# Token rows of attention sent to DRAM from ScalarE's queue instead of SyncE's

## The chip, the cores and the metric

The kernel runs on one core of a Trainium2 chip. The metric is the device time of one execution in microseconds (us). Engines are named PE (TensorE), DVE (VectorE), ACT (ScalarE), POOL (GpSimd) and SP (SyncE); SP computes nothing here, it issues transfers. A transfer issued from SP goes to one hardware queue (q1 in the profile), one issued from ACT to another (q10), one from POOL to a software queue (q0).

## The reference, cut to what matters

Attention with a sigmoid in place of the softmax, then a mixture of experts with one expert per token, then a dense two-layer block:

```python
scores = q @ k.T / sqrt(64) - log(448)         # batch 4, 12 heads, 448 tokens, head size 64
x = sigmoid(scores) @ v                        # -> 1792 tokens of 768
e = argmax(x @ w_gate); g = max of softmax     # 8 experts
x[token] = g * (relu(x[token] @ w1[e]) @ w2[e])  # 768 -> 1024 -> 768
out = relu(x @ w_in)**2 @ w_out                # 768 -> 2048 -> 768
```

## The kernel before

**Three stages.** Attention runs over 24 units, one for each pair of heads in each batch (`units`, numbered n = 0 to 23). Routing then sorts the tokens by expert. The mixture of experts and the dense block follow, with all their weights streamed from DRAM. Routing needs the router's logits of every token, so nothing of the later stages can begin on PE before the last unit's token rows have been projected.

**One unit.** A unit n issues, in program order: the load of unit n+3 (L133, L134, both on SP); four score groups `score` on PE, each followed by a sigmoid on ACT (L158) that frees one of two PSUM buffers; between them the product with v (`av`, L164 and L167) of unit n-1, in steps c = 0, 1, 3, 2; and between step 3 and step 2 a call of `rows` for unit n-2. After step 2 of unit n-1, DVE copies the result out of PSUM (`fin_av`, L171, tile xT). Units also carry DVE and ACT work that packs the dense weights (L90 to L97), stored from POOL (L98).

**`rows`.** PE transposes the finished 128x448 block of a unit to token rows and multiplies it by the router's weights at once (L177, PSUM tile pt, one buffer). ACT copies the result to SBUF (L179, tile xn, two buffers). A transfer writes the token rows to the DRAM tensor x_d (L180: 448 rows of 512 bytes, 224 KB). DVE adds the logits to lg (L183, L185). Because xn has two buffers, the copy L179 for unit m may begin only when the transfer L180 for unit m-2 has landed.

**Order.** The whole program is under a manual schedule: every engine, and every engine's transfer issues, run in program order. On SP an issue that waits therefore holds all issues behind it. Up to unit 20, the load of unit n+3 waits until unit n-1's v has been read, which is the end of unit n. From unit 20 on there are also two loads of 768 KB of expert weights per unit into the same four buffers:

```python
if n >= len(units) - 4:
    rawb.append(rawp.tile([128, 2 * CH], F32, tag="raw", name=f"raw{n}", bufs=4))
    ...
        nc.sync.dma_start(out=raw[c], in_=wm[0, :, len(raw) + c])   # L241
```

The buffer that `raw{n}` takes is that of unit n's own q, k and v, which are last read by `av` in unit n+1. These two loads stand ahead of the call of `rows` for unit n-2 in SP's order.

After unit 23, `rows` for unit 22, the four steps of `av` for unit 23 and `rows` for unit 23 are run, and then routing begins on DVE with a maximum over lg (L304). Tokens of a slot are gathered from x_d by POOL (L446).

Of the kernel before, what the change touches and what calls it, by code (L numbers as in the profile page):

```python
# [20 lines left out]
B, H, S, D = 4, 12, 448, 64  # L21
# [6 lines left out]
CP = 112  # L28
# [28 lines left out]
def moe_kernel(ctx: ExitStack, tc: tile.TileContext, qk, v, wg, wm, w2, out):  # L57
    nc = tc.nc
# [6 lines left out]
    x_d = dram.tile([NT + 128, DM], F32, name="x_d")  # L65
# [41 lines left out]
    with ExitStack() as actx:  # L107
# [65 lines left out]
        def rows(b, j):  # L173
            pt = ps_e.tile([128, 2, 512], F32, tag="pt", name=f"pt_{b}_{j}")
            xn = sp_.tile([128, NC, IW], F32, tag="xn", name=f"xn_{b}_{j}")
            for c in range(NC):
                nc.tensor.matmul(pt[:CP, c // 2, (c % 2) * IW:(c % 2) * IW + IW], xT[b, j][:, c * CP:(c + 1) * CP], iw[:, j, :],  # L177
                                 start=True, stop=True, skip_group_check=True)
            nc.scalar.activation(xn[:CP].rearrange("p (a c) n -> p a (c n)", a=2), pt[:CP, :, :2 * IW], AF.Copy)  # L179
            nc.sync.dma_start(out=x_d[128 + b * S:128 + (b + 1) * S, j * 128:(j + 1) * 128].rearrange("(c p) d -> p c d", p=CP), in_=xn[:CP, :, :128])  # L180
            l = lg[:, b * NC:(b + 1) * NC, :]
            if j == 0:
                nc.vector.tensor_copy(l, xn[:CP, :, 128:])  # L183
            else:
                nc.vector.tensor_tensor(l, l, xn[:CP, :, 128:], op=ALU.add)  # L185
# [6 lines left out]
        def extras():  # L192
            rows(*done.pop(0))
# [240 lines left out]
    with ExitStack() as mctx:  # L434
# [141 lines left out]
        for step in FIRST.split():  # L576
            c = int(step[1])
# [208 lines left out]
```

## Time and profile before

| | |
|---|---|
| median of 3 runs | 1073.06 us (1071.05 to 1073.38) |
| the profiled execution's own time | 1073.23 us |
| its span in the trace | 1071.6 us |
| mean granted clock of PE | 0.981 of full speed |
| attention, first instruction to last logits | 0 to 197.7 us |

The profile names a group of instructions by line, engine and tiles. The span starts with the first instruction; all times of rows are microseconds from there. "[2.33 <-DMA x_d<-xn]" behind a row says that the engine stood idle for 2.33 us just before, until the named thing released it. Granted clock is the share of its full rate that PE was allowed: 1.00 is 2.4 GHz, 0.50 is 1.2 GHz.

### The profile page before, as it was taken

To read this page: it belongs to the slowest core of one execution; us is meant where nothing else is said; L and a number is where in the kernel's file an instruction comes from. 1 tells how busy PE (TensorE), PEld (TensorE's weight loads), DVE (VectorE), ACT (ScalarE), POOL (GpSimd) and SP (SyncE) were. 2 spreads that over 40 slices of the span, in tenths; PEclk is the share of its full clock that TensorE was granted. 3 is DMA by queue.
4 is the path that set the end of the run, shared out by engine and by line. 5 is a ranking of instruction groups with operands and counts; after the bars stand their busy time and mean duration, and the time that the engine had idled before them with its cause. 6 is when DMAs were issued, how large, how long until landed. Compare 5 with 4: busy or idle time off the path is not lost. (4 is left out here: it accounts for less than half of the span.)

```text
span 1071.6 us, 14446 instructions
## 1 busy us (share of the span) xinstructions
PE 1016.4 (95%) x5502; PEld 858.0 (80%) x5502; DVE 631.8 (59%) x565; ACT 639.0 (60%) x757; POOL 188.8 (18%) x132
## 2 busy tenths in 40 slices
PE   7999998179999999999999999999999999999997
PEld 3555554068888888889888889998889988899997
DVE  3777774597888888888885567432432323313351
ACT  5666664367888888888875575225652256522661
POOL 0000000373425344252421000001000010000100
PEclk9999998689999999999999999999999999999999
DMA  8788988466149164614445456534242342422550
GB/s 277 265 296 287 319 296 281 137 255 253 45 164 366 60 228 142 221 45 152 173 133 204 141 211 229 174 98 138 89 148 89 118 147 89 147 89 89 194 190 30
DMA packets 50104, 187.80 MB, mean 175 GB/s; under 512 B 6576, under 2 KB 17328, under 8 KB 47984
## 3 DMA queue, kind: packets, MB, share of 16 engines
q1 hardware_dynamic: 45008, 161.03, 44.0%
q0 software_dynamic: 4944, 25.56, 6.2%
q8 instruction: 45, 0.74, 0.3%
q10 hardware_dynamic: 80, 0.25, 0.1%
q14 instruction: 27, 0.22, 0.1%
HBM read 230.85 MB, written 31.47 MB: 245 GB/s over the span
## 5 line engine op out<-in xcount | busy, mean ns | idle before, releaser
L358 DVE TENSOR_TENSOR wl<-raw,wh 128x1536 fp32r<-128x1536 f32 x126 | 256.2, 2056 | 51.5 <-ACT wh L357 49.1
L357 ACT ACTIVATE wh<-raw 128x1536 fp32r<-128x1536 f32 x144 | 213.7, 1484 | 2.8 <-ACT wh L357 0.2
L358 DVE TENSOR_TENSOR wrl<-raw,wrh 128x1536 fp32r<-128x1536 f32 x43 | 75.6, 1758 | 133.2 <-ACT wrh L357 133.1
L476 PE MATMUL py<-wh,hl 128*128 128x384 f32 x304 | 104.7, 345 | 6.2 <-DVE hl L504 6.2
L158 ACT ACTIVATE a<-sc,bias_s 128x896 f32<-128x896 f32 x96 | 82.9, 915 | 42.8 <-PE sc L154 42.7
L474 PE MATMUL py<-wh,hh 128*128 128x384 f32 x304 | 106.8, 351 | 0.0
L475 PE MATMUL py<-wl,hh 128*128 128x384 f32 x304 | 103.1, 339 | 0.1
L714 PE MATMUL pq<-wrh,sh 128*128 128x384 f32 x296 | 99.9, 338 | 0.0
L358 POOL TENSOR_TENSOR wl<-raw,wh 128x1536 fp32r<-128x1536 f32 x18 | 64.1, 3561 | 201.7 <-ACT wh L357 201.7
L716 PE MATMUL pq<-wrh,sl 128*128 128x384 f32 x296 | 99.4, 336 | 0.0
L715 PE MATMUL pq<-wrl,sh 128*128 128x384 f32 x296 | 99.3, 336 | 0.0
L676 PE MATMUL pp<-yh,wrh 128*128 128x512 f32 (+1 forms) x264 | 95.8, 363 | 2.7 <-PEq L623 2.7
L678 PE MATMUL pp<-yh,wrl 128*128 128x512 f32 (+1 forms) x264 | 95.9, 363 | 0.0
L677 PE MATMUL pp<-yl,wrh 128*128 128x512 f32 (+1 forms) x264 | 95.7, 363 | 0.0
L357 ACT ACTIVATE wrh<-raw 128x1536 fp32r<-128x1536 f32 x43 | 63.8, 1483 | 50.3 <-PE pq L716 43.2
L474 PE MATMUL ph<-wh,xh 128*128 128x512 f32 x228 | 92.6, 406 | 0.3 <-ACT xh L460 0.3
L476 PE MATMUL ph<-wh,xl 128*128 128x512 f32 x228 | 90.6, 397 | 0.0
L475 PE MATMUL ph<-wl,xh 128*128 128x512 f32 x228 | 90.4, 396 | 0.0
L680 ACT ACTIVATE r<-pp 128x512 f32<-128x512 f32 (+1 forms) x64 | 34.8, 544 | 86.2 <-PE pp L678 86.2
L358 DVE TENSOR_TENSOR rl<-raw,rh 128x1536 fp32r<-128x1536 f32 x21 | 36.9, 1759 | 75.8 <-ACT rh L357 75.8
L476 PEld LDWEIGHTS py<-wh,hl 128*128 128x128 f32 x304 | 57.6, 189 | 11.7 <-DVE hl L504 11.7
L164 PE MATMUL po<-a,qkv 128*64 128x448 f32 x288 | 66.2, 567 | 0.0
(168 smaller groups left out, 2047.7 us busy)
## 6 DMA issues: line engine op xcount, KB each, us to landing
raw<-in_wm SPq DMA_DIRECT2D x160, 768.0 KB
raw<-w_d SPq DMA_DIRECT2D x62, 768.0 KB
cs<-in_w SPq DMA_DIRECT2D x11, 1536.0 KB
qkv<-in_qk SPq DMA_DIRECT2D x23, 480.0 KB
w_d<-cd POOLq DMA_DIRECT2D x11, 768.0 KB, 8.8
raw<-in_w SPq DMA_DIRECT2D x5, 1536.0 KB
y_d<-y SPq DMA_DIRECT2D x19, 384.5 KB
qkv<-in_v SPq DMA_DIRECT2D x24, 256.0 KB
```

The costliest lines, as they stand in the source:

```text
L158: nc.scalar.activation(a[:, :n], ps[:, :n, :S], AF.Sigmoid, bias=bias_s, scale=1.0 / math.sqrt(D))
L357: nc.scalar.activation(h, src, AF.Copy)
L358: (nc.gpsimd if pool else nc.vector).tensor_tensor(l, src, f32(h), op=ALU.subtract)
L474: nc.tensor.matmul(ps, lh, rh, start=first, stop=False)
L475: nc.tensor.matmul(ps, lh, rl, start=False, stop=False)
L476: nc.tensor.matmul(ps, ll, rh, start=False, stop=last)
L676: nc.tensor.matmul(pp[:, :N], lh, rh, start=(k == 0), stop=False)
L677: nc.tensor.matmul(pp[:, :N], lh, rl, start=False, stop=False)
L678: nc.tensor.matmul(pp[:, :N], ll, rh, start=False, stop=(k == KD - 1))
L714: nc.tensor.matmul(po[t][:, :384], lh, wc[:, o:o + 384], start=(g == 0), stop=False)
L715: nc.tensor.matmul(po[t][:, :384], lh, wcl[:, o:o + 384], start=False, stop=False)
L716: nc.tensor.matmul(po[t][:, :384], ll, wc[:, o:o + 384], start=False, stop=(g == KF2 - 1))
```

## The change

The 24 transfers of token rows to x_d (L180) are issued from ACT's queue, directly behind the copy L179 that fills xn, and no longer from SP's. Nothing else is different: same size, same shape, same buffers, same place in the program.

```diff
             nc.scalar.activation(xn[:CP].rearrange("p (a c) n -> p a (c n)", a=2), pt[:CP, :, :2 * IW], AF.Copy)
-            nc.sync.dma_start(out=x_d[128 + b * S:128 + (b + 1) * S, j * 128:(j + 1) * 128].rearrange("(c p) d -> p c d", p=CP), in_=xn[:CP, :, :128])
+            nc.scalar.dma_start(out=x_d[128 + b * S:128 + (b + 1) * S, j * 128:(j + 1) * 128].rearrange("(c p) d -> p c d", p=CP), in_=xn[:CP, :, :128])
```

## Rows read from the trace of the kernel before

**Rows 1.** The page: busy time of each engine.

```profile
PE 1016.4 (95%) x5502; PEld 858.0 (80%) x5502; DVE 631.8 (59%) x565; ACT 639.0 (60%) x757; POOL 188.8 (18%) x132
```

**Rows 2.** Waits up to 230 us: who waited, total us, times, longest.

```profile
ACT xn L179 <- DMA x_d<-xn: 21.7, 4, 10.7
...
DVE qkh L141 <- DMA qkv<-in_qk: 6.8, 1, 6.8
```

**Rows 3.** Timeline of an undisturbed unit: start, duration, engine, line, tiles.

```profile
68.05 0.62 ACT L179 ACTIVATE xn<-pt 112x544 f32<-112x544 f32 x1 [0.75 <-ACT a L158]
...
69.72 1.91 ACT L158 ACTIVATE a<-sc,bias_s 128x896 f32<-128x896 f32 x2 [1.05 <-PE sc L154]
...
71.88 0.19 PEld L154 LDWEIGHTS sc<-qkh 64*128 64x128 f32 x2 [0.70 <-ACT a L158]
...
72.67 0.19 PEld L156 LDWEIGHTS sc<-qkh 128*128 128x128 f32 x1 [0.30 <-issue]
```

**Rows 4.** Timeline of SP's issues at the end of attention.

```profile
171.63 0.65 SPq L180 DMA_DIRECT2D x_d<-xn  x1
...
178.90 0.38 SPq L180 DMA_DIRECT2D x_d<-xn  x1
188.97 0.80 SPq L241 DMA_DIRECT2D raw<-in_wm  x2
189.87 7.90 SPq L180 DMA_DIRECT2D x_d<-xn  x3
```

**Rows 5.** Timeline of ACT at the end of attention.

```profile
171.44 0.63 ACT L179 ACTIVATE xn<-pt 112x544 f32<-112x544 f32 x1 [2.33 <-DMA x_d<-xn]
171.97 1.90 ACT L158 ACTIVATE a<-sc,bias_s 128x896 f32<-128x896 f32 x2
...
179.93 0.62 ACT L179 ACTIVATE xn<-pt 112x544 f32<-112x544 f32 x1 [3.73 <-DMA x_d<-xn]
185.45 0.62 ACT L179 ACTIVATE xn<-pt 112x544 f32<-112x544 f32 x1 [4.90 <-DMA x_d<-xn]
196.82 0.62 ACT L179 ACTIVATE xn<-pt 112x544 f32<-112x544 f32 x1 [10.74 <-DMA x_d<-xn]
```

**Rows 6.** Timeline of PE and DVE at the end of attention.

```profile
172.05 1.72 PE L164 MATMUL po<-a,qkv 128*64 128x448 f32 x8
...
173.70 0.19 PEld L154 LDWEIGHTS sc<-qkh 64*128 64x128 f32 x2 [0.70 <-ACT a L158]
...
175.22 0.91 PE L167 MATMUL po<-a,qkv 128*128 128x448 f32 x2
...
175.97 1.09 PE L177 MATMUL pt<-iw,xT 128*112 128x136 f32 x8
...
176.99 0.97 PE L164 MATMUL po<-a,qkv 128*64 128x448 f32 x4
...
180.69 0.62 DVE L171 COPY xT<-po 128x448 f32<-128x448 f32 x1
...
181.46 2.13 PE L177 MATMUL pt<-iw,xT 128*112 128x136 f32 x8 [3.50 <-DVE xT L171]
...
197.47 0.19 DVE L185 TENSOR_TENSOR lg<-lg,xn 112x32 f32<-112x32 f32 x1 [7.87 <-ACT xn L179]
```

**Rows 7.** Line 180: duration of an issue, ns, shortest/median/longest.

```profile
L180 SPq DMA_DIRECT2D x_d<-xn x24: 305/382/956, 26.6 to 197.5; - x24
```

**Rows 8.** Timeline of the start: ACT's one issue, SP's longest.

```profile
0.94 0.56 ACTq L131 DMA_DIRECT2D qkv<-in_qk  x1
...
7.87 3.52 SPq L220 DMA_DIRECT2D cs<-in_w  x1
```

**Rows 9.** Windows of 2 us: engines' busy time, then PE clock, DMA share, GB/s.

```profile
182.00:184.00 2.00, 2.00 (x9) 1.53 (x10) 0.98 (x1) 0.00 (x0) 0.72 (x2) 0.50 0.94 353
...
216.00:218.00 2.00, 1.81 (x4) 1.45 (x5) 1.83 (x3) 2.00 (x4) 0.00 (x0) 0.50 0.95 348
```

**Rows 10.** Timeline after routing: the first gather of token rows.

```profile
207.20 2.41 POOL L446 DMA_INDIRECT xg<-x_d,idx  x1 [1.39 <-DMA raw<-in_wm]
```

## The prediction

> **What bounds the kernel now.** I read the page first, then the list of waits for the attention stage, then the timelines of SP, ACT and PE around the longest waits, and last the granted clock there. The page [rows 1] shows PE busy for 95% of the span, so only what leaves PE idle, or slows it, can be won back. The list of waits up to 230 us [rows 2] has one entry that concerns the moved transfer: the copy L179 waits four times, 21.7 us in total, for x_d to land. VectorE's wait for a q/k load stands there once only, at the start.
>
> The reader is to see three things in the timelines. First, an undisturbed unit is paced by PE: its rows repeat every 7.27 us (71.88 [rows 3] to 173.70 [rows 6] is 101.82 us, 14 units of 7.27), and between the copy L179, which ends at 68.67, and the next sigmoid at 69.72 ACT stands idle for 1.05 us waiting for PE [rows 3]. Second, the four waits lie in a row at the end of attention, at 171.44, 179.93, 185.45 and 196.82, with 2.33, 3.73, 4.90 and 10.74 us of idle ACT ahead of them [rows 5]. Third, SP's order causes them. The copy for unit 21 ends at 180.55 [rows 5], but its transfer is issued at 189.87, straight behind the weight loads that SP could not issue before 188.97 [rows 4], because their buffer is freed by the last `av`. Those 9.3 us are not transfer time: the data lies ready in SBUF and SP stands at another instruction. From issue to the next copy released by it the transfer then takes 171.63 to 179.93 = 8.3, 178.90 to 185.45 = 6.55, and 189.87 to 196.82 = 6.95 us [rows 4, 5].
>
> The last of these waits is on the path that sets the end: the copy for unit 23 cannot start, the logits are complete only after 197.47 [rows 6], and routing, the gathers and all expert work follow from there.
>
> **The change part by part.** *Removed:* 24 issues on SP, about 0.38 us each [rows 7], 9 us in all. SP is not on the path by its busy time, so this alone is worth nothing; SP's loads may be issued some 0.4 us earlier per unit, and nobody waits for them [rows 2]. Worth nothing too.
>
> *Added:* 24 issues on ACT, each behind the copy that it reads. After 21 of them (units 0 to 20) a sigmoid of the next unit is queued. The trace has no issue of this shape on ACT. From below its cost is zero; the nearest rows are the same transfer on SP, 0.31 to 0.96 us [rows 7], and ACT's one issue, 0.56 us [rows 8]. The idle gap of 1.05 us [rows 3] holds all of these, so I take zero, with that idle time as the cover. If the gap were exceeded, a second cover follows: the first pair of sigmoids runs 69.72 to 71.63, and the fourth score group, which needs the second one's buffer, loads at 72.67 [rows 3], 1.04 us later. That this cover is real is seen at 171.97: these sigmoids start 0.43 us late (69.72 plus 14 units is 171.54), held up by the late copy [rows 5], and the third score group still loads on time at 173.70 [rows 6]. So an issue costs PE nothing up to about 2.1 us.
>
> *Moved:* the transfer is issued as soon as its copy has finished. It passes, on SP's side, the loads of q, k and v, the loads of packed weights and, in the last four units, the expert weights with their long waits. No wait on ACT is new except for its own copy. In the middle of attention this gains nothing, since no copy waits there. At the end I replay the order with the rows' own durations. The last PE step before the disturbance, `av` step 2 in unit 23, ends at 176.99 + 0.97 = 177.96, and the projection for unit 21 at 175.97 + 1.09 = 177.06 [rows 6]. Then:
>
> - copy for unit 21: 0.1 after the projection, 0.62 long: 177.78. The transfer that it needs, that of unit 19, was issued at its own copy, two units (14.5 us) before; the longest delay seen is 8.3 us. No wait.
> - DVE: logits 0.19 [rows 6], then xT for unit 22, 0.62: 178.64; PE follows 0.15 later (180.69 + 0.62 to 181.46 [rows 6]): 178.79.
> - projection for unit 22, 1.02 to the next PE step (175.97 to 176.99): 179.81.
> - `av` of unit 23: steps 0 and 1, 1.65 (172.05 to 173.70); step 3, 0.75 (175.22 to 175.97); step 2, 0.97: 183.18 [rows 6].
> - xT for unit 23, 0.67 with its start: 183.85; projection from 184.00, 1.09: 185.09; copy, 0.72: 185.81; last logits at 185.84.
>
> The copy for unit 22, at about 179.9, needs the transfer of unit 20, issued near 170.6: 9.3 us, more than any delay seen. The copy for unit 23, at 185.2, needs the transfer of unit 21, issued near 177.8. By the delays above that lands between 184.4 and 186.1, so the copy waits for 0 to 0.9 us. I take zero, because the three delays were measured on transfers queued behind 1.5 MB of expert weights issued just ahead, and here the transfer is issued before those of its unit.
>
> The last logits thus move from 197.47 to 185.84: **11.6 us**. Of the four waits nothing comes back later: the transfer of unit 23, issued at 185.8, is down by 194.1 at the longest delay; the first gather, at 207.20 now [rows 10], moves to 195.6. The same reckoning is the cover for routing and the expert stage: all that follows hangs on the logits and moves with them. The time is 1073.23 - 11.6 = 1061.6 us by the profiled execution, which is 0.17 above the median: **1061.5 us**.
>
> *The clock.* PE was granted half its rate (0.50, 1.2 GHz) at 182 to 184 [rows 9], after the idle 3.5 us ahead of 181.46, and the same projection took 2.13 instead of 1.09 us [rows 6]. In the replay that idle time shrinks to 0.8 us (177.96 to 178.79), so I count full rate. If the half rate came all the same, the stretch from that projection to the end of `av` would take what it takes now, 181.46 to 188.97 = 7.5 us [rows 4, 6], instead of 4.4: a loss of 3.1. The first expert matmuls also run at half rate now (216 to 218, [rows 9]); they do so after a pause of the same length, and I take no change. If the rate returned at once some 1 us would be won; if 3 us later, some 1.5 lost.
>
> **The rivals.** *B, part of the gain.* The half rate stays (3.1) and the copy for unit 23 waits (0.9): 1061.5 + 4.0 = 1065.5 us, with the later clock 1067. For it speaks that PE still has pauses; against it that the pause shrinks to a quarter.
>
> *C, nothing happens:* the transfers land as late as before, since it is the engines that are full; 1073.1 us. In the 2 us around 183 their share is 0.94 [rows 9], which speaks for it. Against it: the transfer of unit 21 would have to take 18 us from 177.8 to about 196, while the delays are 6.55 to 8.3 us [rows 4, 5]; and the 9.3 us before its issue are SP's.
> The Trainium skill has a rule of this kind ("DMA: Bandwidth & Descriptors", section "Issuing engines are not separate DMA queues"): transfers run on the same 16 DMA engines whoever issues them, so a second issuer saves only the sequencer's time to initiate them. Taken as it stands it would give no change here, as 9 us of SP's issue time are off the path; what it leaves out is the waiting of SP in front of the issue, which the rows show, so I give C little.
>
> *D, slower:* ACT is held by its own issue, in each of the 21 units where a sigmoid follows. SP's longest issue took 3.52 us, early in the stage [rows 8]. If each issue on ACT took that, 3.52 - 2.1 = 1.4 us per unit would reach PE: 30 us, 18 more than the gain gives: 1091.5 us. It decides from 2.65 us per issue on (11.6 / 21 = 0.55 above the cover). Against it: this shape never took more than 0.96 us [rows 7], and ACT's queue carries nothing else.
>
> **How the numbers follow.** A, the full gain, 1060 to 1063.5 us by itself: 0.74. B, between that and 1070: 0.14. C: 0.06. D: 0.06. A change of 0.2%, 2.1 us, is about what a measurement of this kernel can tell from none; A and B are faster by more: 0.88, C the same: 0.06, D slower: 0.06. The range has A with the clock's 1 us on the fast side and rounding, 1059, and B up to 1066.5. It leaves out C, D, B's far end and a little below, not quite 0.2.
>
> **What would show it.** Right: the four waits of L179 for x_d are gone from the list; the issues stand on ACT at 0.3 to 1 us within the idle gap and units still repeat every 7.27 us; PE pauses under 1 us ahead of the projection for unit 22, at clock 1.00; SP's last weight loads are issued near 183 instead of 188.97; the last logits come near 185.8, the first gather near 195.6; after that every stage is as long as before. Wrong: a sigmoid that starts late behind each issue, units longer than 7.27 us; a copy that still waits for x_d at 185; a gather that waits for the last transfer; or a stage behind routing that gives the time back.

## The result and the profile after

The changed kernel takes 1062.04 us (median of 7 runs, 1060.6 to 1067.19) against 1073.06 us (7 runs, 1071.05 to 1073.9): a ratio of 0.9904, 95% interval 0.9885 to 0.9922. The prediction was 1061.5 us, range 1059.0 to 1066.5. The profiled execution took 1062.08 us, its span is 11.1 us shorter. One of the seven runs took 1067.19 us, 5 over the others; why stays open.

First the page of the changed kernel (span, busy time), then the list of waits up to 230 us, which answers to [rows 2]:

```profile
span 1060.5 us, 14396 instructions
...
PE 1013.8 (96%) x5502; PEld 857.5 (81%) x5502; DVE 631.8 (60%) x565; ACT 638.8 (60%) x757; POOL 188.4 (18%) x132
```

```profile
DVE lg L185 <- ACT xn L179: 32.8, 20, 2.9
ACT xn L179 <- PE pt L177: 23.2, 23, 4.8
...
ACT xn L179 <- DMA x_d<-xn: 2.2, 1, 2.2
```

The copy L179 now waits for PE 23 times out of 24. Its entry for x_d has shrunk from 21.7 us in four waits to 2.2 us in one, and that one is a wrong label, as the end of attention will show. The view of line 180 shows what an issue costs on ACT, in ns, shortest, median and longest (before: [rows 7]):

```profile
L180 ACTq DMA_DIRECT2D x_d<-xn x24: 311/311/358, 25.1 to 186.2; - x24
```

An undisturbed unit on ACT, from the timeline (before: [rows 3]):

```profile
68.05 0.62 ACT L179 ACTIVATE xn<-pt 112x544 f32<-112x544 f32 x1 [0.71 <-PE pt L177]
68.70 0.31 ACTq L180 DMA_DIRECT2D x_d<-xn  x1
69.77 1.90 ACT L158 ACTIVATE a<-sc,bias_s 128x896 f32<-128x896 f32 x2 [1.10 <-PE sc L154]
...
75.33 0.62 ACT L179 ACTIVATE xn<-pt 112x544 f32<-112x544 f32 x1 [0.95 <-PE pt L177]
```

The issue stands in the gap in which ACT waits for PE; the sigmoids still start when PE has finished, and the unit still takes 7.28 us. Now the end of attention, PE, DVE and ACT in one timeline (before: [rows 5, 6]):

```profile
176.02 1.09 PE L177 MATMUL pt<-iw,xT 128*112 128x136 f32 x8
...
177.04 0.97 PE L164 MATMUL po<-a,qkv 128*64 128x448 f32 x4
177.15 0.62 ACT L179 ACTIVATE xn<-pt 112x544 f32<-112x544 f32 x1 [0.95 <-PE pt L177]
177.81 0.31 ACTq L180 DMA_DIRECT2D x_d<-xn  x1
...
178.84 1.15 PE L177 MATMUL pt<-iw,xT 128*112 128x136 f32 x8 [0.82 <-DVE xT L171]
...
179.92 1.72 PE L164 MATMUL po<-a,qkv 128*64 128x448 f32 x8
180.02 0.62 ACT L179 ACTIVATE xn<-pt 112x544 f32<-112x544 f32 x1 [2.25 <-DMA x_d<-xn]
...
181.57 1.02 PE L167 MATMUL po<-a,qkv 128*128 128x448 f32 x2
...
182.52 0.97 PE L164 MATMUL po<-a,qkv 128*64 128x448 f32 x4
...
184.31 1.15 PE L177 MATMUL pt<-iw,xT 128*112 128x136 f32 x8 [0.82 <-DVE xT L171]
...
185.50 0.62 ACT L179 ACTIVATE xn<-pt 112x544 f32<-112x544 f32 x1 [4.85 <-PE pt L177]
186.15 0.31 ACTq L180 DMA_DIRECT2D x_d<-xn  x1
186.15 0.19 DVE L185 TENSOR_TENSOR lg<-lg,xn 112x32 f32<-112x32 f32 x1 [1.99 <-ACT xn L179]
...
188.54 0.44 DVE L310 TENSOR_TENSOR_SCAN cum<-seg,ohz 112x136 bf16<-112x136 bf16 x1
```

PE's pause ahead of the projection for unit 22 is 0.82 us and no longer 3.50, and the last logits start at 186.15 where they stood at 197.47: 11.3 us. One label misleads: the copy at 180.02 is put down to x_d. The projection that it reads ended at 178.84 + 1.15 = 179.99, so PE alone explains its start; in experiments e1, e3 and e4 the same idle time at the same place, 2.25 or 2.26 us, carries PE's name.

SP's last weight load (before: 188.97 [rows 4]), PE's clock in the last column but two (before: 0.50 [rows 9]), the first gather (before: [rows 10]) and the first expert matmul, from SP's timeline, the windows and the timelines:

```profile
183.90 1.13 SPq L241 DMA_DIRECT2D raw<-in_wm  x1
```

```profile
182.00:184.00 2.00, 1.49 (x6) 0.20 (x4) 0.46 (x1) 0.00 (x0) 0.66 (x6) 1.00 0.94 275
...
206.00:208.00 2.00, 2.00 (x7) 1.61 (x7) 2.00 (x5) 2.00 (x3) 0.00 (x0) 0.65 1.01 399
```

```profile
195.88 2.41 POOL L446 DMA_INDIRECT xg<-x_d,idx  x1 [1.39 <-DMA raw<-in_wm]
...
205.07 0.79 PE L474 MATMUL ph<-wh,xh 128*128 128x512 f32 x1 [0.26 <-ACT xh L460]
```

The gather is 11.3 us earlier too, the span 11.1.

### The profile page after: what moved, and what is told of

It is laid out like the page before. It is cut to its first block, busy times and chain, and to the rows that moved or that the text cites. A ratio compares the mean times of both kernels' runs of the same rounds, so it can differ in the third digit from the quotient of the medians.

```text
span 1060.5 us, 14396 instructions
## 1 busy us (share of the span) xinstructions
PE 1013.8 (96%) x5502; PEld 857.5 (81%) x5502; DVE 631.8 (60%) x565; ACT 638.8 (60%) x757; POOL 188.4 (18%) x132
```

## The experiments

Three questions were open: which of the 24 transfers carry the gain; whether it is SP's order or the second hardware queue that counts; and how far ACT can be held before PE feels it. Each ratio is to runs of the kernel before taken beside the experiment, with a median of 1071.84 us for e1 to e4 and 1072.68 us for e5 to e8.

**e1 and e2: the last six, the first eighteen.** One kernel sends only the transfers of units 18 to 23 from ACT, the other only those of units 0 to 17.

```diff
-            nc.sync.dma_start(out=x_d[...], in_=xn[:CP, :, :128])
+            (nc.scalar if b * NP + j >= 18 else nc.sync).dma_start(...)   # e1
+            (nc.scalar if b * NP + j < 18 else nc.sync).dma_start(...)    # e2
```

> Only the transfers of units 18 to 23 go to ACT's queue, the first 18 stay on SP. Order theory (SP's issue order at the end of attention holds the transfers, and nothing is won before): the whole gain is there, 1061 to 1063.5 us, last logits near 186.2. Rival, that the gain is spread over all 24 transfers (SP freed of issues, loads earlier): a quarter of it, about 1070 us.

> The complement: units 0 to 17 on ACT's queue, the last six on SP as before. Order theory: no gain, 1072 to 1074 us, the four waits of L179 for x_d back at about 2.3, 3.7, 4.9 and 10.7 us. Rival, spread gain: three quarters of it, about 1065 us.

Measured: e1 1062.19 us, ratio to before 0.9911 (0.9893 to 0.993); e2 1073.3 us, ratio 1.0007 (0.9996 to 1.0018). The last copy on e1's timeline, and the entry in e2's list of waits:

```profile
185.40 0.62 ACT L179 ACTIVATE xn<-pt 112x544 f32<-112x544 f32 x1 [4.85 <-PE pt L177]
```

```profile
ACT xn L179 <- DMA x_d<-xn: 20.9, 4, 8.6
```

All of the gain lies in the last six transfers, none in the first eighteen, though these took three quarters of the issues off SP. The four waits are back in e2, with nearly the sum of before and another split than expected: 3.63, 3.18, 5.52 and 8.59 us. Its last logits start at 196.45, 1.0 us before those of the kernel before, which does not show in the time.

**e3: SP, other order.** All transfers stay on SP; in the last four units the expert weights are issued behind `rows`.

```diff
-            if n >= len(units) - 4:      # raw tiles and their two loads (L241)
-                ...
@@
             if done:
                 extras()
+            if n >= len(units) - 4:      # the same lines
+                ...
             av_step(2)
```

> All transfers stay on SP, but in the last four units the two loads of expert weights are issued behind the token rows' transfer, not ahead of it. Order theory: the transfer no longer stands behind loads that wait for av of its own unit; it is issued about one unit earlier and lands 6 to 8.3 us after its issue, so only the copy for unit 23 still waits, 0.3 to 2 us: 1062.5 to 1064.5 us. Rival, own-queue theory (the gain comes from a second hardware queue, on which the packets pass the 1.5 MB of loads ahead of them): the transfers still stand in one queue behind loads, the waits stay above 4 us for the last copy, 1068 us or more.

Measured: 1064.9 us, ratio 0.9933 (0.9913 to 0.9953). SP's timeline and ACT's last copy:

```profile
177.85 0.81 SPq L255 DMA_DIRECT2D raw<-in_wm  x2
178.75 0.38 SPq L180 DMA_DIRECT2D x_d<-xn  x1
183.33 1.16 SPq L255 DMA_DIRECT2D raw<-in_wm  x2
184.58 4.47 SPq L180 DMA_DIRECT2D x_d<-xn  x2
```

```profile
188.07 0.62 ACT L179 ACTIVATE xn<-pt 112x544 f32<-112x544 f32 x1 [7.57 <-DMA x_d<-xn]
```

The transfer of unit 21 is issued at 178.75 instead of 189.87, and three of the four waits are gone. The last copy still waits, until 188.07, against 185.50 in the changed kernel: 2.6 us later, where at most 2 were expected, and the time is 0.4 us over its range. From issue to copy the transfer takes 188.07 - 178.75 = 9.3 us, longer than any delay of before. So of the 11.3 us by which the changed kernel's last copy is earlier, 8.7 come back by SP's order alone; in the times it is 6.9 us of the 9.7 of e1.

The remaining 2.6 us are the queue's, as the view of DMA packets shows. A transfer is 448 rows of 512 bytes. In the changed kernel, from the issue at 177.81 to 182.6 us, ACT's queue has moved the whole transfer of unit 21 (packets, MB, share):

```profile
q10 hardware_dynamic: 464, 0.23, 21.8%
```

In e3 the weight loads of 177.85 are ahead of it on the same queue. From 179.5 to 183.7 us (first line) no packet of 512 bytes moves; from 183.7 to 187.6 us (second line) 496 - 48 = 448 do:

```profile
DMA packets 224, 1.28 MB, mean 304 GB/s; under 512 B 16, under 2 KB 16, under 8 KB 224
...
DMA packets 718, 1.59 MB, mean 409 GB/s; under 512 B 48, under 2 KB 496, under 8 KB 718
```

The last row is thus down about 8.8 us after the issue on SP's queue and within 4.8 us on ACT's. With 4.8 us even the transfer issued at 178.75 would have been down by 183.6, before the last projection of e3 ended (184.10 + 1.15 = 185.25). Both theories are right in part: the order carries most, a queue of its own the rest.

**e4: SP, old order, four buffers.** Only the buffers of xn change, so that the late transfers have no copy waiting for them.

```diff
-            xn = sp_.tile([128, NC, IW], F32, tag="xn", name=f"xn_{b}_{j}")
+            xn = sp_.tile([128, NC, IW], F32, tag="xn", name=f"xn_{b}_{j}", bufs=4)
```

> All transfers stay on SP in the old order; xn gets four buffers in place of two, so the copy for unit m needs the transfer of unit m-4. Order theory, with the copy's buffer as the only place where the late transfer hurts: all four waits are gone, last logits near 186.2, the first gather does not wait because the transfers of units 21 to 23 are issued from 184 on and land by 194: 1061 to 1064 us. Rival, that the late landing itself would hurt next (gather waits for the last token rows): the gather starts after 197, 1064 to 1068 us; and if the queue of its own is what counts, 1070 us or more.

Measured: 1061.81 us, ratio 0.9909 (0.989 to 0.9928), the time of the changed kernel. SP's timeline, then ACT's last copy and the first gather:

```profile
183.33 1.20 SPq L241 DMA_DIRECT2D raw<-in_wm  x2
184.62 1.68 SPq L180 DMA_DIRECT2D x_d<-xn  x3
```

```profile
185.34 0.62 ACT L179 ACTIVATE xn<-pt 112x544 f32<-112x544 f32 x1 [4.90 <-PE pt L177]
```

```profile
195.73 2.41 POOL L446 DMA_INDIRECT xg<-x_d,idx  x1 [1.39 <-DMA raw<-in_wm]
```

Three transfers are still issued late, at 184.62 and after, on SP and behind the weights, and nothing is lost by it: the gather starts where it does in the changed kernel. What cost 11 us was the copy that waited for its buffer, not the late landing.

**e5 and e6: ACT held longer.** The changed kernel with each transfer issued in four pieces (by 112 tokens) and in eight (each of these in two halves of the partitions).

```diff
-            nc.scalar.dma_start(out=x_d[...], in_=xn[:CP, :, :128])
+            for c in range(NC):          # e6: and for p in (0, CP // 2)
+                nc.scalar.dma_start(out=x_d[128 + b * S + c * CP:..., ...], in_=xn[:CP, c, :128])
```

> As the changed kernel, but each transfer of token rows is issued on ACT in four pieces (one for each 112 tokens). At 0.31 us an issue ACT is held 1.25 us, 0.2 us over the idle gap of 1.05 to 1.1. Cover theory (gap plus about 1.04 us of slack between the sigmoids and the score groups that need their buffers): units stay at 7.27 us, 1061 to 1063.5 us. Rival, that what exceeds the gap reaches PE at once: 0.2 us in each of 21 units, some 4 us, about 1066 us.

> As before with eight pieces (each 112 tokens in two halves of partitions): ACT is held about 2.5 us, sigmoids start some 1.45 us late. Cover theory: 1.04 us of that is hidden, about 0.4 us reaches PE in each of 21 units, 8 us: 1069 to 1072 us. Rival without the second cover: 1.45 us times 21 is 30 us, about 1092 us. If the issue costs ACT nothing whatever its number, 1062 us.

Measured: e5 1066.09 us, ratio 0.9937 (0.992 to 0.9955), 4 us over the changed kernel; e6 1144.87 us, ratio 1.0659 (1.0633 to 1.0686). Two units of e5 on ACT's timeline:

```profile
61.19 0.62 ACT L179 ACTIVATE xn<-pt 112x544 f32<-112x544 f32 x1 [1.04 <-PE pt L177]
61.84 1.80 ACTq L181 DMA_DIRECT2D x_d<-xn  x4
...
68.44 0.63 ACT L179 ACTIVATE xn<-pt 112x544 f32<-112x544 f32 x1
69.10 3.19 ACTq L181 DMA_DIRECT2D x_d<-xn  x4
...
76.90 0.62 ACT L179 ACTIVATE xn<-pt 112x544 f32<-112x544 f32 x1 [1.04 <-PE pt L177]
```

and one of e6, with the view of its line 183 (ns):

```profile
69.58 0.62 ACT L179 ACTIVATE xn<-pt 112x544 f32<-112x544 f32 x1 [1.14 <-PE pt L177]
70.23 3.98 ACTq L183 DMA_DIRECT2D x_d<-xn  x8
...
78.82 0.62 ACT L179 ACTIVATE xn<-pt 112x544 f32<-112x544 f32 x1 [1.04 <-PE pt L177]
```

```profile
L183 ACTq DMA_DIRECT2D x_d<-xn x192: 312/398/1687, 24.9 to 277.6; - x192
```

Both times miss what was expected, and the cover holds. A hold of 1.80 us, 0.7 over the gap, leaves the unit at 68.44 - 61.19 = 7.25 us. One of 3.19 makes it 8.46, 1.19 more; one of 3.98 makes it 9.24, 1.97 more. In both PE loses the hold less 2.0 us (3.19 - 1.19, 3.98 - 1.97). What was mis-sized was the hold: four issues in a row do not take 1.25 us but 1.8 to 3.2, eight 3.4 to 6.0 in place of 2.5. e5's sum is near the rival's number, but the rival's mechanism is refuted by the 7.25. In e6 PE's pauses also lowered its granted clock, to a mean of 0.89 between 20 and 100 us and 0.83 between 100 and 180, where the changed kernel has 1.00. This lengthens units beyond the hold less 2.0: the unit that starts with the copy at 58.40 has a hold of 4.52 us and takes 11.18, 3.9 more instead of 2.5, with the clock at 0.50 between 66 and 68 us. So e6's 83 us are the holds and the clock together, and the runs do not part them.

**e7: POOL's queue.** The changed kernel with the transfer on POOL.

```diff
-            nc.scalar.dma_start(out=x_d[...], in_=xn[:CP, :, :128])
+            nc.gpsimd.dma_start(out=x_d[...], in_=xn[:CP, :, :128])
```

> The transfers of token rows go to POOL's software queue in place of ACT's. Order theory: any queue that is free behind the copy will do; the four waits are gone. POOL's small fills for routing stand behind the last transfer in its order, so the scan over the one-hot rows may wait for them, 0 to 2 us: 1062 to 1065 us. Rival, that POOL's own waits for VectorE's packed weights or its slower issue hold the transfers: above 1066 us.

Measured: 1061.95 us, ratio 0.99 (0.9882 to 0.9917). The end of attention on POOL and DVE:

```profile
186.72 0.19 DVE L185 TENSOR_TENSOR lg<-lg,xn 112x32 f32<-112x32 f32 x1 [1.99 <-ACT xn L179]
...
186.98 0.71 POOL L180 DMA_DIRECT2D x_d<-xn  x1 [4.50 <-ACT xn L179]
...
188.16 0.29 DVE L307 TENSOR_TENSOR eq<-eq,rev 112x128 f32<-112x128 f32 x1 [0.40 <-POOL rev L272]
...
189.60 0.44 DVE L310 TENSOR_TENSOR_SCAN cum<-seg,ohz 112x136 bf16<-112x136 bf16 x1
```

POOL's queue does as well as ACT's. The scan over the one-hot rows starts 2.9 us after the last logits, against 2.4 in the changed kernel (186.15 to 188.54). The expected wait is there, but not at the scan: POOL's fills for routing stand behind the transfer, and DVE waits 0.40 us for one of them, `rev`, three instructions ahead of the scan. These 0.5 us are at the low end of what was expected and do not show in the time.

**e8: work into the remaining pause.** The changed kernel with two steps of the last `av` ahead of the rows of unit 22.

```diff
+        av_step(0)
+        av_step(1)
         extras()
-        for c in (0, 1, 3, 2):
+        for c in (3, 2):
             av_step(c)
         extras()
```

> The changed kernel, with steps 0 and 1 of the last av moved ahead of the token rows of unit 22, so that PE has work in the pause of 0.8 us in which VectorE copies xT of unit 22. The chain of the replay gets shorter by that pause and its restart: last logits about 0.9 us earlier, near 185.2, and 1061 us or just below, which the times alone may not tell from 1062. Rival, that the copy for unit 23 then waits for its transfer instead: no gain.

Measured: 1061.1 us, ratio 0.9888 (0.987 to 0.9906). PE and DVE on its timeline:

```profile
176.81 2.48 PE L164 MATMUL po<-a,qkv 128*64 128x448 f32 x12
...
179.21 1.18 PE L177 MATMUL pt<-iw,xT 128*112 128x136 f32 x8
...
184.71 0.19 DVE L185 TENSOR_TENSOR lg<-lg,xn 112x32 f32<-112x32 f32 x1 [1.99 <-ACT xn L179]
```

The pause ahead of the projection for unit 22 is closed and the last logits come 7.90 us after the step of `av` at 176.81, where the changed kernel takes 186.15 - 177.04 = 9.11: 1.2 us less. It is the fastest of the kernels by its median, but its interval overlaps that of the changed kernel, so the gain is shown in the trace and not in the time.

## Why the prediction was right

*The cause* stands. e2 shows that nothing is won in the middle of attention, e1 that the last six transfers carry all, e4 that it is the copy's wait for its buffer that cost the time, and e3 that most of that wait was SP's order: with the queue unchanged, 8.7 of 11.3 us come back. The other 2.6 need a transfer that does not stand behind the weights on its queue.

*The replay* gave the last logits at 185.84; they came at 186.15. Of the 0.3 us, 0.1 had come up by the end of the projection for unit 22 (179.92, counted 179.81), and 0.2 in step 3 of the last `av`, which took 182.52 - 181.57 = 0.95 us where 0.75 was counted. The copy for unit 23 did not wait for its transfer: it starts 0.04 us after its projection ends (184.31 + 1.15 = 185.46). The reason given for counting no wait there also holds: e3 shows that the long delays were those of a transfer behind the weights.

*The cover on ACT* was put at 2.1 us and measures 2.0. The issue itself was bounded by 0 and 0.96 us and takes 0.31.

*Nothing came back later.* The gather moved by 11.3 us as forecast (195.88, forecast 195.6). From there to the first expert matmul 0.2 us were lost: that moved from 216.19 to 205.07, 11.1 us, and the span is shorter by the same 11.1.

*The clock* stayed at 1.00 in every 2 us from 174 to 186, as counted, and this is a quarter of the gain. The shorter pause of PE gives 3.50 - 0.82 = 2.7 us. From that projection to the end of `av` PE takes 178.84 to 182.52 + 0.97 = 183.49, 4.65 us in place of 7.5 (181.46 to 188.97 [rows 4, 6], partly at 0.50 [rows 9]): 2.9 us. From there to the last logits it is 186.15 - 183.49 = 2.7 us in place of 8.5: 5.8 us, the last wait for x_d.

*Rival C* fell, and with it the plain form of the rule of the Trainium skill ("DMA: Bandwidth & Descriptors", section "Issuing engines are not separate DMA queues") that a second issuer saves only the sequencer's time to initiate a transfer. The bytes were the same, and the issues saved on SP were worth nothing by themselves (e2). Most of what was saved is time in which the sequencer did not initiate but waited, at an instruction that had nothing to do with the transfer; the rest, 2.6 us, is the transfer's place behind the weights on SP's queue (e3).

*Rival D* is a real mechanism with the wrong size: e6 shows it, with the clock's share, at 83 us, from holds of 3.4 to 6.0 us. One issue of 0.31 us is far below the 2.0 us from which PE feels it.

## What to carry to other kernels

Here a transfer's place in its issuer's program mattered more than the duration of its issue. Look for a result that lies ready while its issue stands behind another instruction's wait, and follow what the late landing holds, most often a buffer's next write. Three edits repaired it here equally well (a free queue on ACT, one on POOL, more buffers), and a reordering on the same queue did most of it; what it left was the time that the transfer stood behind larger loads on that queue. Before work is put on a compute engine's queue, add the engine's idle gap and the slack of what follows, and compare this with the time that all issues of one go take in the trace.

## What was not expected

Issues in a row on ACT cost more than a single one. Alone, the issue of the transfer of 224 KB took 0.31 us, 24 of 24 within 0.05 us. Split in four, the view of the line shows a median above that and a few issues far longer:

```profile
L181 ACTq DMA_DIRECT2D x_d<-xn x96: 310/441/1666, 24.8 to 192.3; - x96
```

So cutting a transfer into four did not multiply the hold by four but by 5.8 to 10 (1.80 and 3.19 us against 0.31). In e6 eight issues at their median of 0.398 us would take 3.2 us, and the hold at 70.23 is 3.98: there is time between issues too. What makes an issue long, and what fills the time between them, no run here shows.
